# Spectral mixing and a leaky-ReLU layer: tables on 96 partitions and another order of the head

## The chip, the cores and the metric

The kernel runs on one core of one Trainium2 chip. The metric is the time on the device in microseconds, from the first to the last instruction of the program. The text uses the names of the profile for the engines: PE is TensorE (PEld its weight loads), DVE is VectorE, ACT is ScalarE, POOL is GpSimd, and SP is SyncE, which here issues nearly all DMA transfers.

## The reference

A batch of eight inputs `x` of 3008 rows by 256 columns goes through a two-dimensional Fourier transform, of which the real part is kept. The 24064 rows of the result go through two matrix products with a leaky ReLU of slope 0.01 between them. The two weight matrices come as float64, the input and the output are float32.

```python
def _attn_ref(x):                       # x: (8, 3008, 256)
    X = np.fft.fft(x, axis=1)
    X = np.fft.fft(X, axis=2)
    return X.real.astype(np.float32)

def _moe_ref(x, w_in, w_out):           # w_in: (256, 2048), w_out: (2048, 256)
    h = x @ w_in
    g = np.maximum(0.01 * h, h)
    return (g @ w_out).astype(np.float32)
```

## The kernel before

**What is computed where.** The transform along the 256 columns is never carried out on the data. It is a linear map, so the kernel multiplies it into `w_in` once (`fold_w_in`, L489, result `wf`). The transform along the 3008 rows uses symmetries: rows and columns are added to and subtracted from their mirror images on DVE (`add_mirrors`, `fold_columns`, `fold_halves`), which leaves eight groups of 95 or 94 rows. These are multiplied on PE by tables of cosines and sines and put together by a few additions (`butterfly`, L557). The result is called `mixed`. There is one for each of 16 units: eight batches times two parities of the output row. A cosine part and a sine part belong to each unit. The column at the Nyquist frequency (column 128) is handled apart, for all batches at once, with tiles named `nyx`, `nyz` and `nyq`. It is later spread over all partitions (tile `nb`) and added with one weight for each hidden feature (`wn`).

**The steps.** Each unit is cut into three blocks of 251 output rows (the last may be 250). A step is a pair (block j, hidden group f) with f from 0 to 7. `up(j, f)` (L696) makes the hidden values of 256 features. PE writes two banks, `cos_ps` and `sin_ps`, with four matmuls in all (two in each). DVE adds the Nyquist part with the scalar `wn` (L707) and forms the sum and the difference of the two banks (L711, L712). ACT applies the leaky ReLU (L713). `down` multiplies by `w_out` and accumulates in PSUM over the eight values of f. The first two blocks use a plain form with eight matmuls (`down_plain`, L736). All later blocks use seven matmuls after a few additions of POOL (L720 to L723). A step of a later block thus has eleven matmuls of 251 columns on PE. Each float32 matmul appears as two records.

**The head.** Before these steps can run at full speed, the weights have to be read as float64, turned into float32 and folded, and the first batch has to be mixed. A weight piece is an object of class `Weights` with three stages. `begin` takes two DVE operations on the upper words and two ACT operations (L444 to L447), `mantissa` takes one DVE operation (L452), and `end` takes two (L462, L463). `convert_on(old, new)` (L474) runs the mantissa of one piece, the begin of the next and the end of the first, so that ACT has time for its two. `w_in` comes in pieces of 128 rows by 512 columns and `w_out` in eight pieces of 256 rows. In the kernel before, the first quarter of `w_in` is split once more: 256 columns are converted and folded first (`half`), and the other 256 after the first step.

The first unit is mixed by class `Direct`, with larger tables that need no rotations of the data: `even_rows` and `odd_rows`, each one bank of PSUM for each part, and the form of `butterfly` that is called with `direct=True`. Its tables go to work tiles that are used otherwise later.

**What sets the order.** In the head the order on DVE, PE and SP is the order of the program text (`manual_schedule`). So is that of POOL in the first part of the head, and that of ACT in all of it. Every engine works off its instructions in this order. SP also issues its transfers in this order, and each may first have to wait for a buffer or for the end of an earlier transfer. `keep_warm(n)` (L809) puts n matmuls on a blank tile into PE's queue as filling, each of 256 columns. Steps 0 to 15 are those of the first two blocks, alternately. Their order is written out by hand from L896 on. From step 16 on a loop (L960) runs all further steps, with `down` three steps behind `up`.

**Lines that the steps below name.** The loads of x for batch 0 are at L830 (four pieces: two halves h of the mirrored data, and even and odd row groups, which hold four of the eight groups each). The direct tables are loaded at L843, the feature table at L847, the seq tables at L408, the weight pieces at L430, the angles at L851. `spread_wn` (L503) writes the row `wf[0, 1]` of 128 features as a column of `wn`. It issues one small transfer for each 128 features, in turn on SP and on ACT's queue (L506). The banks of PSUM are of two kinds, with four banks each: `up` (for raised values, products and folds) and `sum` (for sums, filling and some folds). Raw weight pieces use the tags `o`, `e` and `raw`, which have two, two and one buffers.

Of the kernel before, what the change touches and what calls it, by code (L numbers as in the profile page):

```python
# [57 lines left out]
F32 = mybir.dt.float32  # L58
# [6 lines left out]
P = 128  # L65
# [5 lines left out]

KW = [377, 376]
# [19 lines left out]
def row_order():  # L92

    at = np.arange(P)[:, None]
    m = [at, 187 - at, 375 - at, 188 + at]
    s = [8 * at, 8 * at + 4, 4 * m[0] + 2, 4 * m[1] + 2] + [2 * i + 1 for i in m]
    return np.where(at < ROWS - (np.arange(NT) > 0), np.concatenate(s, axis=1), -1)
# [36 lines left out]
def seq_tables():  # L134


    out = np.zeros((4, 2, P, TW[0][1]), np.float32)
    direct_out = np.zeros((2, P, sum(DW)), np.float32)
# [47 lines left out]
def angles():  # L186


    m = np.arange(P)[:, None]
    a = np.pi * np.concatenate([(2 * m + 1) / 752, (2 * m + 1) / 1504, (2 * (187 - m) + 1) / 1504], axis=1)  # L190
    out = np.stack([np.cos(a), np.sin(a)], axis=2) * (m < ROWS - 1)[:, :, None]
    return out.reshape(P, -1).astype(np.float32)
# [43 lines left out]
def tile_fnet_leaky_relu(  # L236
# [25 lines left out]

    def load_x(b):
        t = xp.tile([P, 2, 2, NT, D], F32, tag="x", bufs=1, name="xt")
        for h in range(2):
            nc.sync.dma_start(t[:, h], x[b, :, h])
        return t
# [94 lines left out]
    class Direct:  # L362
# [14 lines left out]
        def odd_rows(self, m):  # L377
            po, n = dft_ps(), KW[1]
            for i in range(4):
                nc.tensor.matmul(po[0:m, 0:n], lhsT=self.src[:, 4 + i], rhs=self.tab[1 + i // 2][0:ROWS, i % 2 * n : (i % 2 + 1) * n],  # L380
                                 start=(i == 0), stop=(i == 3))
            return po
# [15 lines left out]
    nyx = const.tile([P, 2, 2, NT, B], F32, name="nyx")  # L398
    nyz = const.tile([P, 16, B], F32, name="nyz")
    angle = const.tile([P, 6], F32, name="angle")  # L400
# [5 lines left out]
    def load_tab(n, c):  # L406
        t = const.tile([P, TW[c][n % 2]], F32, name=f"tab_{n}_{c}")
# [4 lines left out]
    RAW = "o e raw o e o e raw raw o e raw o e raw o e raw".split()  # L412
# [90 lines left out]
    def spread_wn(f0, n):  # L503

        for q in range(f0 // P, (f0 + n) // P):
            (nc.sync, nc.scalar)[q % 2].dma_start(wn[:, q : q + 1], wf[0:1, 1, q * P : (q + 1) * P])  # L506
# [50 lines left out]
    def butterfly(to, m, part, c, v=nc.vector, direct=False):  # L557


        kw, n = KW[c], KB[c]  # L560
        ab, ev, od = (work.tile([P, w], F32, tag=name, bufs=bufs, name=name)
                      for name, w, bufs in (("ab", KC, 1), ("ev", KC, 2), ("od", 568, 1)))
# [44 lines left out]

        def odd(po):
            if direct:
                if v is not nc.vector:  # L610
                    _, po = copied(po, 0, kw)
                v.tensor_tensor(to[0:m, 0:kw], ev[0:m, 0:kw], po[0:m, 0:kw], op=ALU.add)
                v.tensor_tensor(to[0:m, kw : UW[c]], ev[0:m, 0:kw], po[0:m, 0:kw], op=ALU.subtract)
                return
# [21 lines left out]
        return even, odd  # L636
# [22 lines left out]
    def mix_nyquist(c, banks, v):  # L659
        t = work.tile([P, UW[0]], F32, tag="mix0", bufs=2, name="nyq")  # L660
        for made, bank in zip(butterfly(t, B, 0, c, v, direct=(c == 1)), banks):
            made(bank)
        nc.sync.dma_start(nyq_dram[:, c, 0 : UW[c]], t[0:B, 0 : UW[c]])
        return t
# [8 lines left out]
    def spread_first(rows):  # L673

        c = PARITIES[0]
        t = work.tile([P, UW[0]], F32, tag="nb", bufs=2, name="nb")
        for i in range(2):
            half = slice(i * UW[c] // 2, (i + 1) * UW[c] // 2)
            pt = dft_ps()[:, 0 : UW[c] // 2]
            nc.tensor.matmul(pt, lhsT=one, rhs=rows[0:1, half], start=True, stop=True)  # L680
            nc.scalar.copy(t[:, half], pt)
        spreads[0, c] = t
# [13 lines left out]
    def up(j, f):  # L696
        b, c, at, n, _ = blocks[j]
        fs = hidden_blocks(j, f)
        pt = [up_ps("cos_ps"), up_ps("sin_ps")]
        for blk in range(2):  # L700
            for h in range(2):
                nc.tensor.matmul(pt[blk][:, h * n : (h + 1) * n], lhsT=wf[:, blk, fs[h] * P : (fs[h] + 1) * P],  # L702
                                 rhs=mixed[b, c][blk][:, at : at + n], start=True, stop=True)
        cos = work.tile([P, 2 * CW], F32, tag="cos", bufs=3, name="cos")
# [31 lines left out]
    def down_plain(j, f, halves=(0, 1)):  # L736

        _, _, _, n, first = blocks[j]
        if f == 0 and 0 in halves:
            sums[j] = [ps.tile([P, 512], F32, tag="sum", bufs=4, name="sum_ps") for _ in range(2)]  # L740
# [12 lines left out]
    def down(j, f):  # L753
# [4 lines left out]
        if f == 0:  # L758
            banks = [ps.tile([P, 512], F32, tag="sum", bufs=4, name="sum_ps") for _ in range(4)]
# [49 lines left out]
    def keep_warm(n, columns=2 * P):  # L809

        pt = ps.tile([P, 512], F32, tag="sum", bufs=4, name="sum_ps")
# [3 lines left out]
    with tc.manual_schedule(engines={mybir.EngineType.DVE, mybir.EngineType.PE, mybir.EngineType.SP}):  # L815
        with tc.manual_schedule(engines={mybir.EngineType.Pool, mybir.EngineType.Activation}):
# [8 lines left out]
            t = xp.tile([P, 2, 2, NT, D], F32, tag="x", bufs=1, name="xt")  # L825
# [6 lines left out]
            half = WN // 2  # L832
            w = load_w_in(0, half)
            nc.sync.dma_start(nyx, x_nyq)
            for h in range(2):
                load_rows(h, evens)
# [3 lines left out]
            def load_direct(part, pieces):  # L840
                for i in pieces:
                    at = sum(DW[:i])
                    nc.sync.dma_start(tables[part][i][:, 0 : DW[i]], direct_tab[part, :, at : at + DW[i]])  # L843
# [3 lines left out]
            nc.sync.dma_start(feat_sb, feat_tab.rearrange("(a p) n -> p a n", p=P))  # L847
            load_direct(0, (1, 2))
            load_rows(1, odds)
            load_direct(1, range(3))  # L850
            nc.sync.dma_start(angle, angle_tab)  # L851
            o = load_w_out(0)
            convert(w)
            fold_nyquist()
            differences = work.tile([P, 2 * WN], F32, tag="s", bufs=4, name="differences").rearrange("p (c d) -> p c d", d=P)
# [8 lines left out]
            for h in range(2):  # L864
                add_mirrors(t, h, odds)
                fold_columns(t, h, 0, odds)
                if h == 0:
                    fold_columns(t, h, 1, odds)
            fold_halves(t, 0, 1, odds, differences)
            fold_columns(t, 1, 1, odds)  # L870
            fold_halves(t, 1, 1, odds)
# [123 lines left out]
```

## Time and profile before

| What | Value |
|---|---|
| Median of three runs | 1905.6 us (1905.29 to 1905.88) |
| Span of the profiled execution | 1904.0 us |
| Granted clock of PE | 1.000 |
| PE busy | 1895.9 us |
| DVE busy | 1283.4 us |
| POOL busy | 1122.5 us |
| ACT busy | 504.1 us |
| Moved by DMA | 78.13 MB |
| DMA busy in 0 to 47.6 us (first of 40 slices) | seven tenths, 259 GB/s |

A row of the order in time gives the start in us from the beginning of the span, the duration in us, the engine (or its queue, as SPq), the line, the operation with its output and input tiles, the shapes, the number of instructions that are merged in the row, and in brackets the idle time just before and what ended it. A row of the windows gives the stretch, its length, the busy time of PE, PEld, DVE, ACT and POOL with the number of instructions, the granted clock, the mean busy share of the 16 DMA engines and what they moved in GB/s. In the chain that ended last, shares are of the whole span. The list of transfers gives the size of one: a piece of x for batch 0 has 1024.0 KB, a direct table 282.0 or 376.0 KB, the feature table 256.0 KB, `nyx` 128.0 KB, a seq table 189.0 to 191.0 KB, a piece of `w_out` 512.0 KB, a piece of `w_in` 512.0 KB, or 256.0 KB for those of the first quarter.

### The profile page before, as it was taken

The numbers are of one execution on the slowest core, as the hardware profiler recorded it, in microseconds if no ns is written. First come the engines' busy times: TensorE is split into PE (matmuls) and PEld (weight loads), VectorE is DVE, ScalarE is ACT, GpSimd is POOL, SyncE is SP. The second block draws the span as 40 slices with busy tenths as digits, with TensorE's granted clock in tenths as the row PEclk, the third lists the DMA queues.
The fourth block names the chain that finished last, engine by engine and source line by source line (L and its number), as shares of the span: only waits on it lengthen the run. The fifth ranks groups of instructions, "written<-read, shape, count | busy, mean of one in ns | idle before, by whom it ended". The sixth has DMA issues, their size and how long they took to land.

```text
span 1904.0 us, 25360 instructions
## 1 busy us (share of the span) xinstructions
PE 1895.9 (100%) x9140; PEld 1688.2 (89%) x9140; DVE 1283.4 (67%) x2569; ACT 504.1 (26%) x689; POOL 1122.5 (59%) x1511
## 2 busy tenths in 40 slices
PE   9999999999999999999999999999999999999999
PEld 7889888988889888898888988889888898888988
DVE  7878755596656966569655796557865588556554
ACT  3533222232222322223222232222322223222221
POOL 2127655576555865558655675556755576555554
PEclk9999999999999999999999999999999999999999
DMA  7212000020001100020000200002000020000000
GB/s 259 93 31 108 12 20 22 11 108 12 20 22 56 64 12 31 12 108 12 22 20 12 108 23 12 19 12 108 23 12 20 11 119 12 20 11 23 11 11 22
DMA packets 27740, 78.13 MB, mean 41 GB/s; under 512 B 5072, under 2 KB 18768, under 8 KB 25824
## 3 DMA queue, kind: packets, MB, share of 16 engines
q1 hardware_dynamic: 26464, 76.51, 10.8%
q8 instruction: 73, 1.20, 0.3%
q14 instruction: 51, 0.42, 0.1%
q10 hardware_dynamic: 1152, 0.00, 0.0%
HBM read 51.79 MB, written 24.71 MB: 40 GB/s over the span
## 4 chain that ended last, share of the span: by engine, by line
PE 97%; DVE 1%; DMA 1%; SPq 0%; issue 0%; ACTq 0%; ACT 0%; DVEq 0%
PE sum_ps L765 57%; PE cos_ps L702 17%; PE sin_ps L702 17%; PE dft_ps L553 3%; PE sum_ps L745 2%; DMA xt<-in_x_dram 1%; PE wf_ps L497 0%; PE dft_ps L380 0%; DVE cos L707 0%; ACTq L506 0%; ACT wf L499 0%; DVE g L711 0%; DVE g L712 0%; SPq L843 0%; DVE power L462 0%
## 5 line engine op out<-in xcount | busy, mean ns | idle before, releaser
L713 ACT ACTIVATE g<-g 128x1004 f32<-128x1004 f32 (+1 forms) x384 | 399.2, 1040 | 1098.9 <-DVE g L712 996.0
L707 DVE SCALAR_TENSOR_TENSOR cos<-nb,wn,cos_ps 128x251 f32<-128x251 f32 (+1 forms) x768 | 330.3, 470 | 524.7 <-PE cos_ps L702 524.1
L720 POOL TENSOR_TENSOR s<-g 128x251 f32<-128x251 f32 (+1 forms) x368 | 284.9, 774 | 654.1 <-ACT g L713 654.0
L765 PE MATMUL sum_ps<-s,wt 128*128 128x251 f32 (+1 forms) x2208 | 527.6, 374 | 0.0
L765 PEld LDWEIGHTS sum_ps<-s,wt 128*128 128x128 f32 x2208 | 415.9, 188 | 52.4
L702 PE MATMUL cos_ps<-mix,wf 128*128 128x251 f32 (+1 forms) x1536 | 388.3, 375 | 1.8 <-ACT wf L499 1.8
L702 PE MATMUL sin_ps<-mix,wf 128*128 128x251 f32 (+1 forms) x1536 | 387.6, 374 | 0.0
L765 PE MATMUL sum_ps<-g,wo 128*128 128x251 f32 (+1 forms) x1472 | 372.9, 375 | 0.0
L702 PEld LDWEIGHTS cos_ps<-mix,wf 128*128 128x128 f32 x1536 | 290.9, 190 | 37.0 <-ACT wf L499 2.8
L702 PEld LDWEIGHTS sin_ps<-mix,wf 128*128 128x128 f32 x1536 | 290.4, 189 | 34.7
L721 POOL TENSOR_TENSOR s<-s,g 128x251 f32<-128x251 f32 (+1 forms) x368 | 317.8, 864 | 0.0
L765 PEld LDWEIGHTS sum_ps<-g,wo 128*128 128x128 f32 x1472 | 277.3, 190 | 31.5
L723 POOL TENSOR_TENSOR s<-g,s 128x251 f32<-128x251 f32 (+1 forms) x368 | 277.5, 754 | 28.9
L711 DVE TENSOR_TENSOR g<-cos,sin_ps 128x502 f32<-128x502 f32 (+1 forms) x384 | 259.2, 675 | 42.7 <-DVE cos L707 5.6
L712 DVE TENSOR_TENSOR g<-cos,sin_ps 128x502 f32<-128x502 f32 (+1 forms) x384 | 256.8, 669 | 0.0
L722 POOL TENSOR_TENSOR s<-g 128x251 f32<-128x251 f32 (+1 forms) x368 | 254.0, 690 | 0.0
L765 PE MATMUL sum_ps<-g,wt 128*128 128x251 f32 (+1 forms) x736 | 215.8, 375 | 0.0
L765 PE MATMUL sum_ps<-s,wo 128*128 128x251 f32 (+1 forms) x736 | 215.8, 375 | 0.0
L765 PEld LDWEIGHTS sum_ps<-s,wo 128*128 128x128 f32 x736 | 139.4, 189 | 16.4
L765 PEld LDWEIGHTS sum_ps<-g,wt 128*128 128x128 f32 x736 | 139.8, 190 | 15.8
L776 DVE TENSOR_TENSOR o<-e,sum_ps 128x251 f32<-128x251 f32 (+1 forms) x184 | 67.5, 408 | 8.7 <-ACT e L774 8.7
L553 PEld LDWEIGHTS dft_ps<-tab,xt 95*128 95x128 f32 x480 | 58.3, 192 | 1.4
(119 smaller groups left out, 854.6 us busy)
## 6 DMA issues: line engine op xcount, KB each, us to landing
xt<-in_x_dram SPq DMA_DIRECT2D x14, 2048.0 KB, 13.0
out_dram<-o SPq DMA_DIRECT2D x80, 251.0 KB, 2.3
xt<-in_x_dram SPq DMA_DIRECT2D x4, 1024.0 KB, 10.5
raw<-in_w_out_dram SPq DMA_DIRECT2D x8, 512.0 KB, 4.5
out_dram<-o SPq DMA_DIRECT2D x16, 250.0 KB, 2.3
raw<-in_w_in_dram SPq DMA_DIRECT2D x6, 512.0 KB, 5.0
nb<-nyq_dram SPq DMA_DIRECT2D x8, 376.5 KB, 3.5
nb<-nyq_dram SPq DMA_DIRECT2D x7, 376.0 KB
```

Source lines behind the costliest of these rows:

```text
L553: nc.tensor.matmul(o, lhsT=still, rhs=moving, start=(i == 0), stop=(i == 3), skip_group_check=True)
L702: nc.tensor.matmul(pt[blk][:, h * n : (h + 1) * n], lhsT=wf[:, blk, fs[h] * P : (fs[h] + 1) * P], rhs=mixed[b, c][blk][:, at : at + n], st ...
L707: nc.vector.scalar_tensor_tensor(cos[:, hs], in0=spreads[b, c][:, at : at + n], scalar=wn[:, fs[h] : fs[h] + 1], in1=pt[0][:, hs], op0=ALU ...
L711: nc.vector.tensor_tensor(g[:, 0], cos[:, 0 : 2 * n], pt[1][:, 0 : 2 * n], op=ALU.add)
L712: nc.vector.tensor_tensor(g[:, 1], cos[:, 0 : 2 * n], pt[1][:, 0 : 2 * n], op=ALU.subtract)
L713: nc.scalar.activation(g, g, ACT.Lrelu)
L720: nc.gpsimd.tensor_tensor(s1, a[1][0], a[1][1], op=ALU.add)
L721: nc.gpsimd.tensor_tensor(s2, s1, a[0][0], op=ALU.subtract)
L722: nc.gpsimd.tensor_tensor(s3, a[0][0], a[1][0], op=ALU.subtract)
L723: nc.gpsimd.tensor_tensor(s4, a[0][1], s2, op=ALU.subtract)
L765: nc.tensor.matmul(sums[j][p], lhsT=still[p], rhs=moving[p], start=(f == 0 and i % 2 == 0), stop=(f == NH - 1), skip_group_check=True)
L776: nc.vector.tensor_tensor(to, x, y, op=ALU.add)
```

## The change

- **Partitions.** The tiles and DRAM tensors of x, of the Nyquist column, of the direct tables, the seq tables and the angles have 96 rows (`LOADED`) in place of 128. Rows from 95 on were zeros.
- **First quarter of `w_in`.** It is loaded, converted and folded whole, 512 columns, before the first products. The filling is 16 and 3 matmuls in place of 24, 5 and 3.
- **Loads.** The feature table is loaded between the even x pieces of both halves. The pieces 0, 1 and 2 of `w_out`, the second quarter of `w_in` and all eight seq tables are issued at once behind the direct tables, ahead of the conversion in the text. The list of buffers for the raw pieces is shorter by two.
- **`wn`.** All its transfers are issued by SP.
- **Odd rows.** `Direct.odd_rows` takes a range of columns. The products of 251 columns, the first chunk, come first for both parts, with their sums and differences. Those of the other 125 columns come behind the raising of steps 0 and 2.
- **Nyquist.** The sum and the difference of its first unit move from POOL to DVE. The difference and the second half of its spreading come after step 0.
- **First chunk first.** `up` is split into `raised` (matmuls) and `activate` (the rest). Steps 0 and 2, both of the first block, are raised one after the other. Steps 1 and 3 follow behind `down` of step 0. The order of activations is 0, 2, 1, 3.
- From the conversion of the second quarter's second half on, the order is that of before.

```diff
+LOADED = 96
-    at = np.arange(P)[:, None]
+    at = np.arange(LOADED)[:, None]
...
+    def x_tile():
+        return xp.tile([LOADED, 2, 2, NT, D], F32, tag="x", bufs=1, name="xt")
...
-        def odd_rows(self, m):
-            po, n = dft_ps(), KW[1]
+        def odd_rows(self, m, lo=0, hi=KW[1]):
+            po, n = dft_ps() if m == P else sum_ps(), KW[1]
             for i in range(4):
-                nc.tensor.matmul(po[0:m, 0:n], lhsT=self.src[:, 4 + i], rhs=self.tab[1 + i // 2][0:ROWS, i % 2 * n : (i % 2 + 1) * n],
-                                 start=(i == 0), stop=(i == 3))
+                nc.tensor.matmul(po[0:m, 0 : hi - lo], lhsT=self.src[:, 4 + i],
+                                 rhs=self.tab[1 + i // 2][0:ROWS, i % 2 * n + lo : i % 2 * n + hi], start=(i == 0), stop=(i == 3))
...
-            (nc.sync, nc.scalar)[q % 2].dma_start(wn[:, q : q + 1], wf[0:1, 1, q * P : (q + 1) * P])
+            nc.sync.dma_start(wn[:, q : q + 1], wf[0:1, 1, q * P : (q + 1) * P])
...
-            w = load_w_in(0, half)
+            w = load_w_in(0, WN)
             nc.sync.dma_start(nyx, x_nyq)
-            for h in range(2):
-                load_rows(h, evens)
+            load_rows(0, evens)
+            nc.sync.dma_start(feat_sb, feat_tab.rearrange("(a p) n -> p a n", p=P))
+            load_rows(1, evens)
...
             load_direct(1, range(3))
+            o, o1 = load_w_out(0), load_w_out(1)
+            w1 = load_w_in(WN, WN)
             nc.sync.dma_start(angle, angle_tab)
-            o = load_w_out(0)
+            o2 = load_w_out(2)
+            for c in range(2):
+                for n in range(4):
+                    load_tab(n, c)
             convert(w)
             fold_nyquist()
...
-            keep_warm(24)
+            keep_warm(16)
+            fold_w_in(0, WN, w, "sum")
             even_nyq = nyq.even_rows(B)
-            keep_warm(5)
-            even_cosines = cosine.even_rows(P)
-            fold_w_in(0, half, w, "sum")
-            w, w1 = load_w_in(half, half), load_w_in(WN, WN)
-            nyq = mix_nyquist(1, (even_nyq, nyq.odd_rows(B)), nc.gpsimd)
...
+            made_nyq = butterfly(nyq_t, B, 0, 1, nc.gpsimd, direct=True)
+            made_nyq[0](even_nyq)
+            keep_warm(3)
+            made = [mix(u, part, direct=True) for part in range(2)]
+            even = cosine.even_rows(P)
+            odd_nyq = nyq.odd_rows(B)
+            fold_odds(1)
+            made[0][0](even)
+            made_nyq[1](odd_nyq)
+            made[1][0](sine.even_rows(P))
+            odd = [direct.odd_rows(P, *first) for direct in (cosine, sine)]
+            spread_first(nyq_t, 0)
+            for i in (1, 2):
+                for part in range(2):
+                    made[part][i](odd[part], *first)
             nyq = Rows(nya[:, 0], [nyz], 0, 0)
             nyq.fold_even(nc.gpsimd)
             nyq.fold_odd(nc.gpsimd)
+            raised(*steps[0])
+            raised(*steps[2])
+            odd = [direct.odd_rows(P, *others) for direct in (cosine, sine)]
+            o.begin()
+            activate(*steps[0])
+            o.mantissa()
+            o.end()
+            for part in range(2):
+                for i in (1, 2):
+                    made[part][i](odd[part], *others)
+            made_nyq[2](odd_nyq)
+            store_nyquist(1, nyq_t)
...
             down(*steps[0])
+            spread_first(nyq_t, 1)
+            o1.begin()
+            raised(*steps[1])
+            raised(*steps[3])
+            activate(*steps[2])
             convert_on(o1, w1[0])
+            activate(*steps[1])
             down(*steps[2])
+            activate(*steps[3])
+            o3, w2 = load_w_out(3), load_w_in(2 * WN, WN, (0,))
+            convert_on(w1[0], w1[1])
+            down(*steps[1])
             convert_on(w1[1], o2)
```

## The prediction

> **What bounds the kernel now.** The page first: the table of busy times and the chain of work that ended last.
>
> ```profile
> PE 1895.9 (100%) x9140; PEld 1688.2 (89%) x9140; DVE 1283.4 (67%) x2569; ACT 504.1 (26%) x689; POOL 1122.5 (59%) x1511
> ...
> PE 97%; DVE 1%; DMA 1%; SPq 0%; issue 0%; ACTq 0%; ACT 0%; DVEq 0%
> ```
>
> TensorE bounds the kernel, but its 100% includes the fill-up matmuls of L813, and the 3% of the chain that is not PE lies in the first 80 us. So I read that stretch in order of time, then its DMA by windows.
>
> ```profile
> 10.60 3.57 SPq L843 DMA_DIRECT2D direct<-in_direct_tab_dram  x3
> 10.61 1.23 DVE L274 TENSOR_TENSOR xt<-xt 128x1024 f32<-128x1024 f32 x1 [3.34 <-DMA xt<-in_x_dram]
> ...
> 16.41 0.33 SPq L851 DMA_DIRECT2D angle<-in_angle_tab_dram  x1
> ...
> 19.83 0.56 SPq L506 DMA_DIRECT2D wn<-wf  x1
> ...
> 21.48 1.23 DVE L274 TENSOR_TENSOR xt<-xt 128x1024 f32<-128x1024 f32 x1 [2.12 <-DMA xt<-in_x_dram]
> ...
> 32.63 0.85 DVE L707 SCALAR_TENSOR_TENSOR cos<-nb,wn,cos_ps 128x251 f32<-128x251 f32 x2
> ...
> 56.65 1.40 ACTq L506 DMA_DIRECT2D wn<-wf  x2
> ...
> 58.51 1.11 PE L702 MATMUL cos_ps<-mix,wf 128*128 128x251 f32 x4 [0.79 <-ACT wf L499]
> ...
> 59.66 0.86 DVE L707 SCALAR_TENSOR_TENSOR cos<-nb,wn,cos_ps 128x251 f32<-128x251 f32 x2 [2.53 <-PE cos_ps L702]
> ...
> 79.78 1.11 PE L702 MATMUL cos_ps<-mix,wf 128*128 128x251 f32 x4 [0.60 <-ACT wf L499]
> ```
>
> ```profile
> 5.00:10.00 5.00, 5.00 (x25) 4.39 (x24) 2.10 (x5) 1.20 (x3) 1.57 (x3) 1.00 0.90 294
> 10.00:15.00 5.00, 4.63 (x25) 3.46 (x23) 4.32 (x5) 0.00 (x0) 0.00 (x0) 1.00 1.03 411
> 15.00:20.00 5.00, 5.00 (x27) 4.42 (x26) 4.33 (x7) 0.37 (x1) 0.00 (x0) 1.00 1.03 412
> ```
>
> To be seen: VectorE waits for x until 21.48; the first up step reaches VectorE at 32.63; VectorE then carries the head until TensorE waits last, at 79.78. The last two columns are DMA share and GB/s: full from 10 us on. SP starts its 12th load (10.60) when the 4th lands (10.61), and the 15th (16.41) when the 7th lands, so it has at most eight transfers out. After 79.78 PE works without gaps, so **the end moves by what that PE start moves.** Useful PE work before it is 58.4 us (eight up steps of 1.70 and six and a half down steps of 3.40, from the spacing of their rows; the second and third quarter's folds and half the first's, 8.6; the products and first half-fold of the head, 14.1); 21.4 us are lost to waits and filler.
>
> [...] No 96-row load is in this trace. [...] The trace shows the price: ACT copies nothing while it issues (1.40 us at 56.65). [...] here L290 rises from 0.68 to 1.35 us beside GpSimd at 25.5.
>
> **The change, part by part.**
>
> *Loads.* Sizes in KB of the issue list. Calibration: 163 and 294 GB/s over the first two 5 us move 2231 KB by 10 us, then 402 KB per us (412 GB/s). A load lands when everything ahead of it and itself, plus 800 KB, has moved: 4th load, 1664 KB, 10.6; 7th, 3994 KB, 16.4; 11th (last of x), 6026 KB, 21.45. So landing = 10 + (S - 1431)/402. On 96 rows the x pieces are 768 instead of 1024, the direct tables 211 and 282, seq tables 142; the first quarter's two loads grow from 256 to 512. If time follows bytes, S is 1888, 2912, 3892, 5224 for the four x pieces: landings 11.1, 13.7, 16.1, 19.4. The last is 2.0 us sooner.
>
> *VectorE up to the mixing.* Converting 512 columns twice costs 5.2 us in place of 3.7 at the start. The two loads, first in line, have moved by about 6 us, so this ends near 10.5, before x lands: it costs nothing. The second half-quarter's conversion (3.1 us of VectorE between 32.2 and 41.7) disappears. Chain: 11.1 + 2.54, wait, 13.7 + 2.54 + 1.2 + 2.54 (odd rows h=0) = 20.0, then 3.8 to 23.8. The direct butterflies: even parts 2 x 1.15, Nyquist sum moved from POOL to VectorE 0.5, four 251-column pieces 1.6: 28.2. TensorE, with whole fold 3.43 and products in hand, raises step 0 by 29.5. Then `o.begin` 0.7. [...] first `cos` could start at about 29.7.
>
> *The wn loads, moved.* Here is a new wait. `spread_wn` is now on SP only, and SP must first issue o, o1, w1 (two), angle, o2 and eight tables: five times 512 and 8 x 142 KB, which before came later. wn's first column is the 29th transfer, so it waits for the 21st, the first table: S = 8704, 10 + (8704 - 1431)/402 = 28.1. It then queues behind the other tables, all moved by 28.6, with up to 2.0 us for the 800 KB lag. With the 2.2 us least landing time of L506, I take 30.8 for column 0 and 31.3 for column 1 (issue 0.5 later); bounds 29.5 and 32.5. Queued behind that VectorE instruction are o's conversion, the second odd pieces and all later activations. So `cos` is bound by wn at 30.8, against 32.63; the pair's second ends at 31.8 and `g` at 33.1, against 34.85.
>
> *The rest of the head.* VectorE from 33.1: o's mantissa and end 1.9 (35.0), 125-column pieces 4 x 0.27 and Nyquist difference 0.5 (36.6), o1.begin 0.7, step 2's activation 2.14 (from 85.69 to 87.83), conversion 2.6 (to 90.43), two activations 4.28, two conversions 5.2: 51.5. TensorE runs beside it: down(0) 35.1 to 38.5, spread 0.65, raises until 42.9 (the first waits for step 2's activation, since only four banks hold raised results), down, down, half a down 8.5: 51.4. So the second quarter's fold begins at 51.5, against 54.2: 2.7 us sooner with the same work behind it. The split products have the same columns; their extra weight loads cost at most 0.7 us in PE's idle stretch near 34, bounded by 0 and 0.7.
>
> *ACT's DMA issues, removed.* At this fold, PE to next up took 4.3 us (54.2 to 58.51), of which 3.43 is PE; without 1.40 us of issuing on ACT the copies end with the fold. wn column 5 now comes 0.55 later on SP and takes some back: VectorE gains 0.5, PE 0.8. At the third quarter's fold the PE start is bound at 79.0 by the half down ahead of it instead of 79.78. VectorE is 3.15 us early there (2.7 + 0.5), PE 0.75 more: **3.9 us** in sum. Later folds had PE busy and gain nothing. The x loads of later batches, 13.0 us to landing, are hidden by some 190 us of matmuls; so is combine_w_out on POOL. Sum: 1904.0 - 3.9 = 1900.1 for the profiled span; the timed runs lie 1.6 above it, so 1901.7.
>
> **Rivals.**
> - *[...]no bytes saved:* 96 rows take 128 rows' time. Through the last table 5859 KB go to 96 rows; a third more is 1953 KB, 4.9 us on wn. [...] That eats the gain of 3.9: [...]1906.6, I take 1906.0. [...] Against: nothing in the trace.
> - *A quicker start:* wn is no longer last. The first 10 us move 2231 KB where the full rate from 3 us on would move 2814; that is 1.5 us. A quarter fewer x rows[...] may help. Then VectorE at 29.7 is the bound, 1.1 us sooner: with the second column's lag gone too, 1900.2. Against: the slow start is unexplained.
> - *Slower: wn stalls VectorE.* [...] 96-row loads are slower still. Break-even: the 5859 KB take 14.6 us at 402 KB per us, and with 3.9 more (wn at 34.7 instead of 30.8) the gain is gone, at 324 GB/s. At 250 GB/s, about what 5 to 8 us show (229, 279 and 246 in its three us), they take 9.4 more: wn at 40.2, and 1905.6 + 5.5 = 1911.1. Everything behind `cos` on VectorE waits with it. For: SP's order is fixed, so nothing passes wn. Against: share 1.03 at 412 GB/s shows engines that can be kept full.
>
> **How the numbers follow.** Bytes saved 0.50 (own range 1900.2 to 1903.4), quicker start 0.21, [...]slower 0.14. A measurement of this kernel tells 0.2%, 3.8 us, from no change: faster means below 1901.8. My forecast is just inside that line; the terms left out (fewer conversions competing, PE filler shortened from 32 to 19 matmuls) point down, so 0.37 of its 0.50 goes below. Faster 0.37 + 0.21 = 0.58, same 0.13 + 0.15 = 0.28, slower 0.14. The range, 1898.2 to 1906.8, leaves out most of the slower case and a little below the quicker one.
>
> **What would show it.** Right: last x piece lands near 19.4, wn column 0 near 31 with VectorE waiting on DMA wn for 1 us, second fold at about 51.5, no PE wait after 76. Wrong: x landing at 22 or later[...]; no wait on wn (the order isn't what I read); a PE wait on PSUM banks longer than my 0.3 us after down(0), or a fold later than 54.

## The result: 1916.6 us, and the profile after

The changed kernel takes **1916.6 us** (median of four runs, 1916.44 to 1917.67) against 1905.7 us of the kernel before: a ratio of 1.0059, with an interval of 1.0041 to 1.0076. It is slower by about 11 us, 0.6%, where 1901.7 us and a gain had been forecast. The profiled span is 1915.9 us against 1904.0.

First the page of the changed kernel: busy times with shares of the span, the chain that ended last by engine, and from the list of transfers the large loads of x (number, KB of each, median us from issue to landing).

```profile
PE 1901.5 (99%) x9118; PEld 1686.3 (88%) x9118; DVE 1282.2 (67%) x2565; ACT 501.4 (26%) x681; POOL 1101.3 (57%) x1509
...
PE 92%; DVE 4%; DMA 2%; issue 1%; SPq 0%; DVEq 0%
...
xt<-in_x_dram SPq DMA_DIRECT2D x14, 1536.0 KB, 12.7
```

PE is still the bound, but its share of the last chain fell from 97% to 92%, and those of DVE (from 1% to 4%) and DMA (from 1% to 2%) rose. A load of x for a later batch has a quarter fewer bytes than before (1536 in place of 2048 KB), and the list still gives it 12.7 us to land, where it gave 13.0. The list mixes the two halves of x; the half that DVE reads first even came later, as shown below.

The next view shows why: windows of 5 us of the changed kernel (stretch, length, busy time of PE, PEld, DVE, ACT and POOL, clock, DMA share, GB/s).

```profile
10.00:15.00 5.00, 4.46 (x12) 1.80 (x10) 3.54 (x5) 1.03 (x2) 0.00 (x0) 1.00 1.04 232
15.00:20.00 5.00, 3.73 (x23) 2.89 (x24) 4.46 (x6) 0.84 (x3) 3.01 (x4) 1.00 1.04 237
20.00:25.00 5.00, 2.65 (x8) 0.58 (x8) 2.35 (x4) 0.00 (x0) 2.44 (x7) 1.00 1.04 233
...
35.00:40.00 5.00, 5.00 (x13) 3.60 (x12) 1.41 (x5) 2.58 (x7) 0.39 (x2) 0.50 0.56 125
```

The DMA share is full (1.04), as it was before (1.03), but it carries 232 to 237 GB/s in place of 411 and 412. The DMA is as busy as before and moves little more than half as much. From 20 to 25 us PE works for 2.65 us only, and from 30 to 40 us its clock is at 0.50.

In order of time, the rows of the changed kernel that answer to those of before:

```profile
24.32 1.22 DVE L282 TENSOR_TENSOR xt<-xt 96x1024 f32<-96x1024 f32 x1 [2.62 <-DMA xt<-in_x_dram]
...
26.34 8.07 SPq L417 DMA_DIRECT2D tab<-in_seq_tab_dram  x8
34.68 2.48 SPq L515 DMA_DIRECT2D wn<-wf  x4
...
39.47 0.86 DVE L734 SCALAR_TENSOR_TENSOR cos<-nb,wn,cos_ps 128x251 f32<-128x251 f32 x2 [3.60 <-DMA wn<-wf]
...
60.30 3.66 PE L506 MATMUL wf_ps<-win,feat_sb 128*128 128x512 f32 x12
...
84.20 1.01 PE L725 MATMUL cos_ps<-mix,wf 128*128 128x251 f32 x4
```

The last piece of x lands at 24.3 (before: 21.5). SP needs 8.07 us to issue eight tables, 5.9 us of it in seven waits for earlier landings, and reaches `wn` at 34.68. The first `cos` starts at 39.47, after a wait of 3.60 us for `wn` (before: 32.63). The second quarter's fold starts at 60.30 (before: 54.11). The raising behind the third quarter's fold starts at 84.20, without the wait on ACT that stood there before, when it started at 79.78. The head thus ends 4.4 us late.

The other 7.6 us are lost later. These are the issues of x for the batches 1 to 3, first in the kernel before, then in the changed one:

```profile
150.54 0.82 SPq L266 DMA_DIRECT2D xt<-in_x_dram  x2
381.44 0.81 SPq L266 DMA_DIRECT2D xt<-in_x_dram  x2
612.31 0.81 SPq L266 DMA_DIRECT2D xt<-in_x_dram  x2
```

```profile
154.86 0.81 SPq L274 DMA_DIRECT2D xt<-in_x_dram  x2
386.45 0.81 SPq L274 DMA_DIRECT2D xt<-in_x_dram  x2
618.53 0.81 SPq L274 DMA_DIRECT2D xt<-in_x_dram  x2
```

Their distance is the period of a batch: 230.90 and 230.87 us before, 231.59 and 232.08 after. The first issue is 4.3 us late, and each batch adds 0.7 to 1.2 us. DVE's first addition to x of batch 1, before and after:

```profile
157.79 2.29 DVE L274 TENSOR_TENSOR xt<-xt 128x2048 f32<-128x2048 f32 x1 [1.08 <-DMA xt<-in_x_dram]
```

```profile
164.22 2.29 DVE L282 TENSOR_TENSOR xt<-xt 96x2048 f32<-96x2048 f32 x1 [3.20 <-DMA xt<-in_x_dram]
```

It starts as soon as its half of x has landed: 7.25 us behind the issue before, 9.36 us after, so a quarter fewer bytes took 1.3 times as long. The addition itself takes 2.29 us on 96 rows as on 128. The waits of the changed kernel (total us, times, longest) name the chain:

```profile
DVE xt L282 <- DMA xt<-in_x_dram: 28.2, 10, 3.7
PEld sum_ps L792 <- DVE o L803: 7.4, 14, 1.0
PE sum_ps L792 <- DVE o L803: 3.2, 5, 0.6
```

Seven of the ten waits on x, 23.6 us in all, lie behind 150 us. While DVE waits for x, the additions that write the output (L803) stand behind it in its queue. They free the PSUM banks into which PE sums, so PE and its weight loads wait for them. Ahead of the runs the reading was: **data come at a lower rate on 96 rows; that delays the head by way of `wn`, and every later batch by way of DVE's queue.** The rival readings were that the new order of the head is to blame, or the shortened filling, which let PE's clock drop.

### The profile page after: what moved, and what is told of

Read it like the earlier page. It is cut to its first block, busy times and chain, and to the rows that moved or that the text cites. A ratio compares the mean times of both kernels' runs of the same rounds, so it can differ in the third digit from the quotient of the medians.

```text
span 1915.9 us, 25297 instructions
## 1 busy us (share of the span) xinstructions
PE 1901.5 (99%) x9118; PEld 1686.3 (88%) x9118; DVE 1282.2 (67%) x2565; ACT 501.4 (26%) x681; POOL 1101.3 (57%) x1509
## 4 chain that ended last, share of the span: by engine, by line
PE 92%; DVE 4%; DMA 2%; issue 1%; SPq 0%; DVEq 0%
PE sum_ps L792 54%; PE cos_ps L725 16%; PE sin_ps L725 16%; PE sum_ps L772 3%; PE dft_ps L562 3%; DVE g L738 1%; DVE xt L282 1%; DVE cos L734 1%; DVE g L739 1%; DMA direct<-in_direct_tab_dram 1%; PE wf_ps L506 1%; DMA xt<-in_x_dram 0%; DVE xt L291 0%; DMA tab<-in_seq_tab_dram 0%; DMA feat_sb<-in_feat_tab_dram 0%
## 5 line engine op out<-in xcount | busy, mean ns | idle before, releaser
L747 POOL TENSOR_TENSOR s<-g 128x251 f32<-128x251 f32 (+1 forms) x368 | 275.5, 749 | 681.0 <-ACT g L740 681.0
L725 PEld LDWEIGHTS cos_ps<-mix,wf 128*128 128x128 f32 x1536 | 292.2, 190 | 35.7 <-issue 1.6
L748 POOL TENSOR_TENSOR s<-s,g 128x251 f32<-128x251 f32 (+1 forms) x368 | 313.3, 851 | 0.0
L749 POOL TENSOR_TENSOR s<-g 128x251 f32<-128x251 f32 (+1 forms) x368 | 247.2, 672 | 0.0
L792 PEld LDWEIGHTS sum_ps<-g,wt 128*128 128x128 f32 x736 | 139.8, 190 | 15.8
L803 DVE TENSOR_TENSOR o<-e,sum_ps 128x251 f32<-128x251 f32 (+1 forms) x184 | 67.4, 408 | 8.7 <-ACT e L801 8.7
## 6 DMA issues: line engine op xcount, KB each, us to landing
xt<-in_x_dram SPq DMA_DIRECT2D x14, 1536.0 KB, 12.7
```

Of the source, the lines that this page charges most:

```text
L747: nc.gpsimd.tensor_tensor(s1, a[1][0], a[1][1], op=ALU.add)
L748: nc.gpsimd.tensor_tensor(s2, s1, a[0][0], op=ALU.subtract)
L749: nc.gpsimd.tensor_tensor(s3, a[0][0], a[1][0], op=ALU.subtract)
L792: nc.tensor.matmul(sums[j][p], lhsT=still[p], rhs=moving[p], start=(f == 0 and i % 2 == 0), stop=(f == NH - 1), skip_group_check=True)
L803: nc.vector.tensor_tensor(to, x, y, op=ALU.add)
```

## The experiments

**Rows and order taken apart.** The changed kernel on 128 rows, and the kernel before on 96:

```diff
-LOADED = 96
+LOADED = 128
```

> The order of the changed kernel, with 128 rows everywhere instead of 96. Theory 1 (the 96-row loads are the loss: 232 GB/s at a DMA share of 1.04 against 412 before, which delays wn in the head and makes DVE wait for x in the seven later batches): the later 7.6 us vanish, and wn's first column lands near 34.8 instead of 39, so the time is 1905.2, between 1903 and 1907. Theory 2 (the order is the loss: the shorter filling lets PE's clock fall to 0.5 and the moved loads delay wn): the time stays above 1909.

Measured: **1906.95 us**, a ratio to before of 1.0006 (0.9998 to 1.0015). Of the changed kernel's 11 us, 9.7 go with the rows. The rest of the change, on 128 rows, is level with the kernel before within the interval. Its rows in time show why it gains nothing:

```profile
28.01 1.76 SPq L417 DMA_DIRECT2D tab<-in_seq_tab_dram  x3
30.02 3.07 SPq L515 DMA_DIRECT2D wn<-wf  x4
```

```profile
35.12 0.86 DVE L734 SCALAR_TENSOR_TENSOR cos<-nb,wn,cos_ps 128x251 f32<-128x251 f32 x2 [6.48 <-DMA wn<-wf]
```

DVE is done with the mixing at 28.6 and then waits 6.48 us for `wn`, which SP issues behind the tables even at full rate.

The kernel before on 96 rows (the sizes of its tiles and DRAM tensors alone, in the old order):

```diff
+LOADED = 96
-        t = xp.tile([P, 2, 2, NT, D], F32, tag="x", bufs=1, name="xt")
+        t = xp.tile([LOADED, 2, 2, NT, D], F32, tag="x", bufs=1, name="xt")
...
-    nyx = const.tile([P, 2, 2, NT, B], F32, name="nyx")
+    nyx = const.tile([LOADED, 2, 2, NT, B], F32, name="nyx")
```

> The kernel before, with 96 rows for x, Nyquist, tables and angles and nothing else changed. Theory 1: four x pieces and three tables ahead of the last x piece at 232 GB/s instead of 412 put it 4.2 us later (25.7 us), the head loses about that, and the seven later batches lose 1.1 us each on PE: 1905.6 + 4.2 + 7.6 = 1917.4, between 1914 and 1919. Theory 2: 96 rows cost next to nothing by themselves, 1904 to 1907.

Measured: **1924.1 us**, 1.0099 (1.0084 to 1.0114). That is 18.5 us more than before, and 6.7 more than I had expected. The rate was low here too (195 GB/s from 15 to 20 us), and the last piece of x came later still, at 27.86. Then PE's clock fell:

```profile
20.00:25.00 5.00, 4.10 (x17) 2.11 (x16) 2.01 (x3) 1.10 (x3) 0.67 (x3) 1.00 1.05 234
...
30.00:35.00 5.00, 5.00 (x11) 3.19 (x11) 3.30 (x8) 0.24 (x1) 1.89 (x4) 0.50 0.88 293
```

The products of the odd rows, first in the kernel before, then on 96 rows:

```profile
24.59 2.76 PE L380 MATMUL dft_ps<-direct,differences 95*128 95x376 f32 x8 [0.43 <-DVE differences L290]
...
27.19 2.69 PE L380 MATMUL dft_ps<-direct,xt 95*128 95x376 f32 x8
```

```profile
31.30 5.25 PE L381 MATMUL dft_ps<-direct,differences 95*128 95x376 f32 x8
36.34 5.22 PE L381 MATMUL dft_ps<-direct,xt 95*128 95x376 f32 x8
```

The same work takes about twice as long, and the first `cos` starts at 46.44 in place of 32.63: 6.4 of these 13.8 us are the later x, and some 5 us are the slower products. My forecast had only the first of the two.

The four cases give: old order 1905.6 on 128 rows and 1924.1 on 96; new order 1906.95 and 1916.6. On 96 rows the new order is 7.5 us better than the old one, on 128 rows 1.3 us worse. So the rows are the loss. In the old order they do more harm, since there the products of PE at its lower clock stand on the path to the first `cos`.

**The order of SP's transfers alone.** The kernel of 1906.95 us, with `o2` and the eight tables issued behind the first `wn` transfers:

```diff
             w1 = load_w_in(WN, WN)
             nc.sync.dma_start(angle, angle_tab)
-            o2 = load_w_out(2)
-            for c in range(2):
-                for n in range(4):
-                    load_tab(n, c)
...
             fold_w_in(0, WN, w, "sum")
+            o2 = load_w_out(2)
+            for c in range(2):
+                for n in range(4):
+                    load_tab(n, c)
```

> As e1_after_128, with the third w_out piece and the eight seq tables issued behind the wn transfers of the first quarter instead of ahead of them. If wn waits only because SP issues those loads first: wn lands at about 30.5, VectorE's own chain (31 to 32) becomes the bound of the first activation, and the time is 3 us below e1_after_128, about 1902, faster than the kernel before. If wn is not what holds the first activation there: same as e1_after_128 within 1 us.

Measured: **1899.75 us** (median of 20 runs), 0.9981 (0.9973 to 0.9988), and faster than both kernels. Twelve of the runs took 1899.4 to 1899.9 us, eight took 1904.5 to 1906.3; the last experiment comes back to the eight. `wn` goes out ahead of the tables, and `cos` starts 6.4 us sooner:

```profile
20.93 3.60 SPq L515 DMA_DIRECT2D wn<-wf  x4
...
26.70 4.35 SPq L417 DMA_DIRECT2D tab<-in_seq_tab_dram  x5
```

```profile
28.76 0.86 DVE L734 SCALAR_TENSOR_TENSOR cos<-nb,wn,cos_ps 128x251 f32<-128x251 f32 x2 [0.47 <-DMA wn<-wf]
```

The folds start at 49.58, 68.35 and 88.76, against 56.91, 75.69 and 96.09: 7.3 us sooner each. So on 128 rows the place of `wn` behind the tables cost 7.2 us between the medians (the eight longer runs lie only 0.6 to 2.5 us under 1906.95), and it held back all that the rest of the new head had gained.

**The filling.** The changed kernel with twelve more filling matmuls, so that PE does not idle between 20 and 30 us:

```diff
             fold_w_in(0, WN, w, "sum")
+            keep_warm(2)
...
             even = cosine.even_rows(P)
+            keep_warm(3)
             odd_nyq = nyq.odd_rows(B)
+            keep_warm(7)
```

> The changed kernel (96 rows) with 12 more filling matmuls in the places where PE waits in its head (2, 3 and 7). Theory 1 (wn binds the first activation at 39.5 us, and PE's fall to half its clock between 27 and 40 us lies beside that wait): clock 1.00 throughout, but the time falls by at most 1.5 us, to 1915 to 1917. Theory 2 (the clock is the loss of the head): the first products and the two raised steps finish 4 us sooner and the time falls by 3 to 5 us, to 1912 to 1913.5.

Measured: **1916.85 us**, 1.0062 (1.0045 to 1.0079), the time of the changed kernel. The clock was held where it had fallen before:

```profile
25.00:30.00 5.00, 5.00 (x28) 4.55 (x27) 4.86 (x12) 0.24 (x1) 0.00 (x0) 1.00 1.05 374
30.00:35.00 5.00, 5.00 (x23) 3.77 (x21) 2.77 (x9) 2.41 (x7) 0.39 (x2) 1.00 1.06 299
```

The first `cos` started 0.8 us sooner, at 38.66, since it still waited for `wn` (5.29 us now). The second quarter's fold was at 60.32, as at 60.30 without the filling. The lower clock lay beside the wait for `wn` and cost nothing there. As the cause of the loss by itself it is out; that it would cost nothing once `wn` comes sooner isn't shown by this run.

**The later batches alone.** The 1899.75 us kernel, with x of the batches 1 to 7 alone on 96 rows:

```diff
-        t = x_tile()
+        t = xp.tile([96, 2, 2, NT, D], F32, tag="x", bufs=1, name="xt")
         for h in range(2):
-            nc.sync.dma_start(t[:, h], x[b, :, h])
+            nc.sync.dma_start(t[:, h], x[b, 0:96, h])
```

> As e3_after_128_wn_first, with only the x loads of batches 1 to 7 on 96 rows (the tile too). If the later loss of the changed kernel (7.6 us behind its head, 5.6 in e2_before_96, 6.3 in e4_after_filled) is the slower x of the later batches and nothing of the head: 1899.75 + 6.5 = 1906.3, between 1905 and 1908, and the start of the third fold near 68.3 us as in e3. If the later loss comes from the head (buffers or banks in another phase): within 1 us of e3.

Measured: **1905.3 us**, 1.0003 (0.9994 to 1.0011): 5.55 us more than on 128 rows, of which 0.7 us is in the head (the last of its three folds starts at 89.44 in place of 88.76) and about 5 us behind it. Here x keeps its 128 rows in DRAM and only 96 of them are read, and the load is slow all the same: the half that DVE reads first landed 9.06 us behind the issue in batch 3 (from 607.64 to 616.70), about as in the changed kernel (9.36) and not as on 128 rows (7.25). So it isn't the layout of x in DRAM. The loads that the forecast called hidden cost about 0.7 us a batch.

**The head's rows with `wn` first.** The changed kernel on 96 rows, with the transfers in the order of the 1899.75 us kernel:

```diff
-            o2 = load_w_out(2)
-            for c in range(2):
-                for n in range(4):
-                    load_tab(n, c)
...
             fold_w_in(0, WN, w, "sum")
+            o2 = load_w_out(2)
+            for c in range(2):
+                for n in range(4):
+                    load_tab(n, c)
```

> The changed kernel (96 rows) with the third w_out piece and the seq tables issued behind the first wn transfers. wn then lands near 29 us instead of 37 to 39; but PE at half clock raises step 0 only by about 37.4. So the first activation moves by 2.1 us, and the time from 1916.6 to 1914.5, between 1913 and 1916: less than the gain on 128 rows (7.2), since the slow loads and the clock hold the head there. If wn were the only wait of that head: 1909 to 1911.

Measured: **1916.25 us** (four runs, 1912.15 to 1917.07), 1.0053 (1.0038 to 1.0068). In the profiled execution the first `cos` came 3.4 us sooner, at 36.05, and the second fold 3.1 us sooner, at 57.23; that execution was the fastest of the four, 1912.15 us. The other three (1915.50 to 1917.07) took about as long as without the edit. In the profiled one `cos` no longer waited for `wn`. The clock of PE was 0.50 from 30 to 35 us: DVE waited 2.49 us for products, and `cos` started 0.1 us behind the four records of its raising, which took 2.04 us (33.90 to 35.94) where they took 1.11 us in the 1899.75 us kernel. So on 96 rows the wait for `wn` and the slow head (late x, then PE at half its clock) lie side by side: taking away either one alone, here or with the filling, leaves the median where it was. Both together weren't run, and what the other three executions lost isn't seen.

**`wn` in turn on SP and ACT.** The 1899.75 us kernel, with the issue of before:

```diff
-            nc.sync.dma_start(wn[:, q : q + 1], wf[0:1, 1, q * P : (q + 1) * P])
+            (nc.sync, nc.scalar)[q % 2].dma_start(wn[:, q : q + 1], wf[0:1, 1, q * P : (q + 1) * P])
```

> As e3_after_128_wn_first, with the wn transfers in turn on SP and ACT's queue, as in the kernel before. The prediction put the price of ACT's issuing at 0.8 us of PE at the second quarter's fold and 0.75 at the third's: 1900.5 to 1901.3. If a wn column on SP alone, landing 0.55 us later, costs as much: the same as e3 within 0.4 us.

Measured: **1902.0 us**, 0.9989 (0.9982 to 0.9996): 2.3 us more, where 0.75 to 1.5 had been expected. The waits of PE on ACT are back, of the same length as in the kernel before (rows of an execution of 1908.0 us; 14 of the 20 runs took 1901.6 to 1902.5):

```profile
60.48 1.11 PE L725 MATMUL cos_ps<-mix,wf 128*128 128x251 f32 x4 [0.79 <-ACT wf L508]
81.76 1.11 PE L725 MATMUL cos_ps<-mix,wf 128*128 128x251 f32 x4 [0.60 <-ACT wf L508]
```

Keeping `wn` off ACT is worth 2.3 us, of which these two rows show 1.4; where the rest lies isn't shown.

**What row counts do to the rate.** The 1899.75 us kernel with a different cut of x's rows in each batch. The batches 1 to 7 are loaded in pieces that end at these rows; a batch with two numbers has two transfers for each h:

```diff
+        cuts = {1: (96,), 2: (112,), 3: (64, 96), 4: (128,), 5: (32, 64, 96), 6: (48, 96), 7: (80, 96)}[b]
+        t = xp.tile([cuts[-1], 2, 2, NT, D], F32, tag="x", bufs=1, name="xt")
...
+            for lo, hi in zip((0,) + cuts, cuts):
+                nc.sync.dma_start(t[lo:hi, h], x[b, lo:hi, h])
```

> As e3_after_128_wn_first, with the x of each later batch loaded in other row cuts: batch 1 96 rows, 2 112 rows, 3 64 + 32, 4 128, 5 three times 32, 6 twice 48, 7 80 + 16. To be read: GB/s while each load runs. [...] Theory B[...]: 112, 96, 48 and 80 all near 230[...]. If the row count did not matter: 412 for all.

Measured: 1903.3 us (one run). One window out of each batch's loads, in the order 96, 112, 64+32, 128 and three times 32 rows:

```profile
145.00:150.00 5.00, 5.00 (x25) 4.50 (x24) 4.29 (x9) 0.54 (x2) 3.02 (x4) 1.00 1.06 256
...
377.00:382.00 5.00, 5.00 (x26) 4.49 (x24) 4.55 (x9) 0.17 (x2) 2.97 (x4) 1.00 0.94 282
...
614.00:619.00 5.00, 5.00 (x26) 4.49 (x25) 2.12 (x4) 1.41 (x2) 2.60 (x4) 1.00 1.12 239
...
845.00:850.00 5.00, 5.00 (x25) 4.50 (x24) 4.18 (x4) 0.82 (x1) 4.10 (x3) 1.00 0.98 417
1071.00:1076.00 5.00, 5.00 (x25) 4.51 (x24) 4.40 (x9) 0.35 (x1) 2.78 (x4) 1.00 1.03 226
```

In these windows of one program, on one chip, 128 rows move at 417 GB/s and all others at 226 to 282. Had 112 rows taken as long as 128, their rate would have been about 365 (7/8 of 417), and it was 256 to 282; that is out. A second probe tried other cuts, 120 and 104 undivided rows among them:

```diff
-        cuts = {1: (96,), 2: (112,), 3: (64, 96), 4: (128,), 5: (32, 64, 96), 6: (48, 96), 7: (80, 96)}[b]
+        cuts = {1: (120,), 2: (104,), 3: (64, 128), 4: (88, 96), 5: (32, 64, 96, 128), 6: (72, 96), 7: (96, 128)}[b]
```

> The order with the wn transfers first on 128 rows, with x of the batches 1 to 7 loaded on other rows: 120, 104, 64+64, 88+8, three times 32 and then 32, 72+24, and 96+32. The first seven-batch probe moved 112 rows at 256 to 282 GB/s and 96 rows at 220 to 256 GB/s, against 374 to 417 for 128, so the rate isn't set by the share of rows alone. [...] Theory B: any load on fewer rows than 128 is slow in itself: 120 and 104 rows stay at 220 to 290 GB/s, as 112 and 96 did. Time: 1900 to 1905 us under both, not decisive.

Windows of the batches with 120, 104 and 64+64 rows:

```profile
145.00:150.00 5.00, 5.00 (x26) 4.48 (x25) 4.19 (x9) 0.65 (x2) 3.02 (x4) 1.00 0.97 210
...
389.00:394.00 5.00, 5.00 (x26) 4.49 (x25) 0.00 (x0) 1.00 (x1) 2.60 (x4) 1.00 0.80 170
...
622.00:627.00 5.00, 5.00 (x25) 4.50 (x24) 4.39 (x9) 0.45 (x2) 3.02 (x4) 1.00 0.99 213
```

If these loads took as long as one of 128 rows at 412 GB/s, 120 rows would move at 386 GB/s and 104 at 335 (estimates from that rate, by the number of rows); measured were 210 and 170. Theory B expected 220 to 290, so both lie below its range too. A lower DMA share explains this only in part: it was 0.97 with 120 rows and 0.80 with 104, and 170 / 0.80 = 213 GB/s for a full share is the rate of 64+64 rows (213 at 0.99), half of that of 128 rows in one piece (417 at 0.98). The time, 1917.0 us (one run), lay outside the 1900 to 1905 us that I had expected, and most of the excess comes from the two undivided loads: the batches with 120 and 104 rows had periods of 238.6 and 238.3 us.

The size of the packets isn't the reason either. From the issue of x for batch 1 on, the trace of the kernel before has 258 packets of 8 KB or more (150 to 167 us) and that of the changed kernel 193 (154 to 172 us). That is close to twice 128 and twice 96: in both kernels one packet of 16 KB for each row of the two halves.

**A slow load that costs nothing.** The probes showed one more thing. The batches with 64+32, 48+48, 64+64, 88+8 or 72+24 rows kept the period of 230.9 us, at the same low rates. So the changed kernel was run with each later load of x cut into two of 48 rows:

```diff
-            nc.sync.dma_start(t[:, h], x[b, :, h])
+            for lo, hi in ((0, 48), (48, LOADED)):
+                nc.sync.dma_start(t[lo:hi, h], x[b, lo:hi, h])
```

> The changed kernel with each load of x for the batches 1 to 7 cut into two of 48 rows. In the two probes the batches whose loads were cut in two (64+32, 48+48, 64+64, 88+8, 72+24) kept the period of 230.87 us of a batch at the same low rate of 160 to 240 GB/s, since the planned order put the first addition of x two or more steps further back in DVE's queue, while undivided loads of 96 rows, with that addition one step behind their issue, took 231.6 to 232.1 us. Theory A (the loss of 7.6 us in the later batches is DVE's queue waiting for a slow load, and not the load itself): the period is 230.9 us again, and the time 1916.6 - 7.6 = 1909.0 us (1908 to 1910), with no wait of DVE for x behind 100 us. Theory B (the slow load costs that time wherever it is read): 1915 to 1917 us.

Measured: **1909.7 us**, 1.0023 (1.0014 to 1.0033), 6.9 us less than the changed kernel. Batch 1 in order of time, first in the changed kernel, then with the cut loads:

```profile
160.35 0.67 DVE L739 TENSOR_TENSOR g<-cos,sin_ps 128x500 f32<-128x500 f32 x1
164.22 2.29 DVE L282 TENSOR_TENSOR xt<-xt 96x2048 f32<-96x2048 f32 x1 [3.20 <-DMA xt<-in_x_dram]
166.43 0.85 DVE L734 SCALAR_TENSOR_TENSOR cos<-nb,wn,cos_ps 128x250 f32<-128x250 f32 x2
```

```profile
162.19 0.86 DVE L735 SCALAR_TENSOR_TENSOR cos<-nb,wn,cos_ps 128x250 f32<-128x250 f32 x2 [2.32 <-PE cos_ps L726]
...
166.84 0.86 DVE L735 SCALAR_TENSOR_TENSOR cos<-nb,wn,cos_ps 128x251 f32<-128x251 f32 x2 [2.39 <-PE cos_ps L726]
...
169.01 2.28 DVE L283 TENSOR_TENSOR xt<-xt 96x2048 f32<-96x2048 f32 x1
```

With undivided loads the first addition of x stands one step behind their issue in DVE's queue, and `cos` of the next step waits behind it. With the cut loads the planned order puts it two steps further back, and it waits for nothing. The cut loads are as slow as the undivided ones (220 GB/s from 160 to 165 us; 226 undivided). Thus the loss in the later batches isn't the slow load as such but the place of its first reader in DVE's queue. Cutting into more pieces doesn't help further: three and four times 32 rows had periods of 232.8 and 233.2 us. Why isn't known.

**The best order with filling.** The 1899.75 us kernel, with two filling matmuls on either side of the even rows' sine products:

```diff
+            keep_warm(2)
             made[1][0](sine.even_rows(P))
+            keep_warm(2)
```

> The order with the wn transfers first on 128 rows, with two filling matmuls ahead of the even rows' sine products and two behind them. The times of that order without them fell into two groups, 1899.4 to 1899.9 and 1904.5 to 1906.3 us. Theory A: the upper group is executions in which the clock of PE halves between 25 and 35 us since PE idled too much between 20 and 25 us (in the profile of the order with wn on both queues the idle time there was 1.66 us and the clock 0.50 afterwards; in the one with all wn on SP it was 0.53 us and the clock stayed at 1.00). Then the filling, 4 matmuls of 0.26 us of which 0.53 us are idle time anyway, costs at most 0.5 us: lower group 1899.5 to 1900.1 us, and the upper group is gone or rarer. Theory B: the groups come from something else: both remain in like shares, at 0 to 0.5 us more each.

Measured: **1899.7 us** (six runs, 1899.55 to 1899.85), 0.9968 (0.9956 to 0.9980). The filling costs nothing, and no run lay in the upper group. That the clock goes with the group shows in all 20 runs without the filling: the mean clock of the whole execution was 0.996 or 0.997 in the eight of the upper group and 0.999 or 1.000 in the twelve others. With the filling PE no longer idles there:

```profile
20.00:25.00 5.00, 5.00 (x26) 3.98 (x25) 4.40 (x9) 0.24 (x1) 1.98 (x6) 1.00 1.05 408
25.00:30.00 5.00, 5.00 (x23) 3.78 (x22) 4.85 (x16) 1.76 (x6) 0.40 (x2) 1.00 0.98 318
```

This is the best version found, 6.2 us under the 1905.9 us of the kernel before on the same chip. Six runs don't prove that the upper group is gone: 8 of 20 were in it without the filling, and by chance six would miss it about once in 21 times (0.6 to the sixth power).

## Why the prediction was wrong

Two steps failed. The forecast span was 1900.1 us and the measured one 1915.9. Of these 15.8 us, 8.3 lie in the head (PE's start at 84.20, for which the forecast amounts to 79.78 - 3.9 = 75.9) and the rest, 7.5, in the later batches. Two of the signs that the prediction named for being wrong came: x landed later than 22, and the second fold began later than 54.

**Loads: wrong.** This is the step that failed in the head. "If time follows bytes" put the last piece of x at 19.4 and the full rate at 412 GB/s. On 96 rows the rate was 232 to 237 GB/s at a full DMA share, and the piece came at 24.3. Time did not follow bytes: at these rates 25% fewer bytes take about a third longer (0.75 × 412 / 233 = 1.33). The estimate used one rate for both row counts, though no 96-row load was in the trace.

**Order of SP: right in kind.** That `cos` would be bound by `wn`, and that DVE would stand ready at about 29.7 before it, was right: at full rate on 128 rows DVE was ready at 28.6 and `wn` came at 35.1. The rival "no bytes saved" (rated at 0.15) is that same kernel in its arithmetic: `wn` 4.9 us later than 30.8, so at 35.7, and 1906.0 us; measured 35.1 and 1906.95. The chain of landings therefore held to a microsecond once the rate was right. What the text didn't ask is what the head would give with `wn` ahead of the tables: 7.2 us on 128 rows.

**Rest of the head: right in sum, beside an offset.** The second fold came 8.8 us behind the forecast of 51.5 and the first `cos` 8.7 us behind that of 30.8. What was worked out between the two points thus held as a sum. Within it, two errors made up for each other in part: the conversion behind step 2's activation took 4.0 us (47.52 to 51.49, with 1.29 us of waiting for ACT) in place of 2.6, but the fold at 60.30 didn't wait for the end of the last conversion (60.97), as the forecast had it.

**ACT's issues: right, too small.** PE's waits on ACT vanished, as forecast. The changed kernel made up 6.2 - 4.4 = 1.8 us between the second fold and 84.20, against the 1.2 us of the text. Measured by itself, on 128 rows, the edit is worth 2.3 us.

**"The x loads of later batches are hidden": wrong.** This is the second step that failed. They were set beside 190 us of matmuls, but the reader of a load is DVE, which takes the first addition of x one step later. Each of the seven waits there was up to 3.7 us long and cost PE 0.7 to 1.2 us, 7.6 us in sum, nearly as large as the loss in the head. The wait was already in the trace of before, 1.08 us at 157.79, short enough for PE not to notice. With the addition two steps further back, 6.9 us came back.

**Filling: wrong sign, no cost.** The shortened filling was said to point down. The clock fell to 0.50 in the changed kernel, and more filling held it at 1.00; but it fell beside the wait for `wn`, where it cost nothing.

**The rivals.** The rival on the slower side, rated at 0.14, was right in kind: "96-row loads are slower still", priced at 250 GB/s with `wn` at 40.2; measured were 232 to 237 GB/s and 39.5. That the times agree so well is in part luck: at 233 GB/s its own sum gives 42.0, and the changed kernel made up for it at 341 and 347 GB/s from 25 to 35 us. Its sum of 1911.1 us lacks the later batches: in spans, 1904.0 + 4.3 in the head + 7.6 behind it = 1915.9. **Why** a load on each other count that was tried takes 1.5 to nearly 3 times as long for each byte (417 GB/s against 282 to 147) stays open; shown is that the number of bytes, the layout of x in DRAM and the size of the packets aren't it, and that a lower DMA share isn't it on 96 rows (1.04 at 232 to 237 GB/s).

## What to carry to other kernels

Fewer rows in a transfer didn't make it shorter here (9.36 us to landing on 96 rows, 7.25 on 128): before a tile is cut from 128 rows, measure one load with the new row count, and read its DMA share beside its GB/s; the sign here was a share of 1.04 at 232 to 237 GB/s, where 128 rows had 1.03 at 412. Beside 190 us of matmuls the later loads of x were still not hidden, since DVE's queue waited up to 3.7 us for them and PE lost 7.6 us; so look at what stands behind the first reader, not at how much other work there is. Small transfers that gate the first step go ahead of bulk loads in the queue that issues them: here that was worth 7.2 us on 128 rows, and without it the reordering gained nothing. On 96 rows the same move left the median where it was, since another wait stood beside it: a wait is worth only what the next one leaves.

## What the runs showed of the hardware that wasn't expected

- In windows of 5 us inside a load, loads of x of 16 KB for each row ran at 374 to 419 GB/s with 128 rows (DMA share 0.88 to 0.99) and at 147 to 282 GB/s with 112, 96, 80+16, 64+32, 48+48 or 32+32+32 rows (0.88 to 1.12). With 120 rows they ran at 200 to 216 (0.94 to 1.00) and with 104 at 170 to 174 GB/s (0.74 to 0.81).
- Runs of the 1899.75 us kernel fell into two groups, 1899.4 to 1899.9 (12 of 20) and 1904.5 to 1906.3 us. With `wn` on both queues the profiled execution was of such an upper group (1908.0 us), and its clock of PE showed 0.81 and then 0.50, beside only 3.34 us of PE work from 20 to 25 us:

```profile
20.00:25.00 5.00, 3.34 (x14) 2.40 (x13) 4.31 (x8) 0.24 (x1) 1.97 (x6) 0.81 1.04 406
25.00:30.00 5.00, 5.00 (x14) 3.87 (x12) 2.42 (x9) 0.00 (x0) 0.00 (x0) 0.50 1.05 373
30.00:35.00 5.00, 5.00 (x11) 3.02 (x10) 2.60 (x7) 2.58 (x7) 0.39 (x2) 0.50 0.66 211
```

  An idle PE alone isn't enough for it: in the first probe PE worked 3.43 us in that stretch and kept its clock at 1.00. Some 1.6 us of idle time there is a margin that sometimes holds and sometimes doesn't, at a price of 5 to 7 us. Four filling matmuls of 0.26 us each took the idle time away for nothing.
